# Mixing the first batch's k and v once at full width, in one-bank tiles emptied by two engines, in a new order

## Chip, cores, metric

One core of one Trainium2 chip. The metric is the device time of one execution in microseconds (us); most executions of one kernel agree within 0.3%. An execution is called slow when it is over 1.5% above the fastest of the same kernel, and such executions are left out of every comparison.

Engines in the profile: PE is TensorE (matmuls), PEld its weight loads, DVE is VectorE, ACT is ScalarE, POOL is GpSimd, SP is SyncE. PSUM is the memory that matmuls write, in banks of 512 fp32 columns.

## The reference

Four batches of eight heads, 768 positions, 64 per head. Every head's k and v are mixed over eight blocks of 96 positions by an 8x8 matrix `P` that five rounds of exp and normalisation make; block-local attention follows; its output goes through a bilinear feed-forward part.

```python
for _ in range(5):
    P = np.exp(P - P.max(-1, keepdims=True))
    P = P / P.sum(-1, keepdims=True);  P = P / P.sum(-2, keepdims=True)
k_sorted = einsum('bhij,bhjcd->bhicd', P, k_blocks)     # the same for v
attn = softmax(scale * q_block @ k_sorted_block.T)      # within a block of 96
x = (attn @ v_sorted_block), heads side by side         # [3072, 512]
out = ((x @ w_a) * (x @ w_b)) @ w_out                   # 512 -> 1536 -> 512
```

## The kernel before

The feed-forward matmuls of one batch run while the attention of the next is made in the gaps between them ("units" between "steps"). Only batch 0 has no feed-forward work beside it, so its attention is made in two halves (blocks 0 to 3, then 4 to 7): the first half alone, in the startup; the second half between the first feed-forward steps. Each half mixes k and v of a head pair on its own:

```python
def half_mix(h, hp, what, eng, fill=0, cols=512):       # h: half, hp: pair of heads
    ...
    mix = psF.tile([P, 512], FP32, tag="F", name="mixh")
    keep_busy(mix, fill, cols)                           # filler matmuls
    for c in range(NCH):                                 # 6 chunks of 128 positions
        for e in range(2):                               # the two heads
            nc.tensor.matmul(<64 partitions, 64 columns of mix>,
                lhsT=src2[:, e, c * D:(c + 1) * D],
                rhs=s_all[:, 2 * hp + e, h * NBH:(h + 1) * NBH], start=True, stop=True)
    copy(eng, <kT or vT>, mix)                           # one engine, 128x384

# startup, order on TensorE (cut)
half_mix(0, 0, "k", "act", fill=2, cols=256); half_mix(0, 0, "v", "dve")
to_columns(1)
half_mix(0, 1, "k", "act")
half_scores(0, 0); half_v(0, 0)
half_mix(0, 1, "v", "dve"); half_mix(0, 2, "k", "act", fill=1)
half_o(0, 0); half_scores(0, 1); half_v(0, 1)
...
# second half, between feed-forward steps (cut)
def M(hp): half_mix(1, hp, "k", "act"); half_mix(1, hp, "v", "act")
def R(hp): half_scores(1, hp); half_v(1, hp)
```

`s_all` holds the mixing weights (P times a mask). `half_scores` makes q times k and an Exp on ScalarE, `half_v` turns (transposes) v, `half_o` makes the output and normalises it on VectorE, `half_x` turns that for the feed-forward part. At the end of the startup five "early products" (`begun`) do three of the four accumulations of the first feed-forward tiles, and the first steps only close them. `psF` has four one-bank buffers, `psA` two of two banks. On TensorE, GpSimd and SyncE the program's order is kept; outside the startup the instructions of ScalarE and VectorE are placed by a scheduler.

The softmax here doesn't subtract the row's maximum and nothing guards it: scores larger than these inputs give would overflow.

## Time and profile before

| | before |
|---|---|
| time, median of the first 3 runs | 243.91 us (243.35 to 244.25) |
| span of the profiled run | 241.7 us |
| TensorE busy | 97% of the span, clock full |
| from the permutations' end (`P` is ready and TensorE begins to turn it) to the first closing matmul (startup) | 11.66 us |
| from there to batch 1's first matmul (dense stretch) | 21.43 us |

The table cuts the span where the argument cuts it. TensorE is busy in both stretches; the difference is that in the startup each step waits for the one before it, while in the dense stretch feed-forward matmuls fill whatever time is left. How to read the views, and the lines themselves, are in the prediction.

### The profile page before, as it was taken

The page shows a single profiled execution, that of the slowest core. Times are in us where ns is not written, and L with a number is a line of the kernel's source. Part 1 is how long each engine was busy: PE and PEld are TensorE (multiplying, and loading weights), DVE is VectorE, ACT ScalarE, POOL GpSimd, SP SyncE. Part 2 cuts the span into 40 slices and gives each one's busy share as a digit, 9 for nine tenths or more (in the row PEclk, how much of TensorE's full clock was granted, in tenths as well). Part 3 has the DMA queues.
Part 4 walks back from the last instruction along what each step waited for, and adds up shares of the span by engine and source line. Part 5 has one row for each costly group of instructions (what it writes and reads, how often), then busy time and mean ns, then how long its engine had stood idle before and what let it go on. Part 6 is the DMA issues. An engine that isn't in the chain of part 4 may idle for free.

```text
span 241.7 us, 5392 instructions
## 1 busy us (share of the span) xinstructions
PE 235.4 (97%) x2179; PEld 140.2 (58%) x2189; DVE 109.1 (45%) x258; ACT 104.1 (43%) x198; POOL 70.4 (29%) x97
## 2 busy tenths in 40 slices
PE   7999999999999999999999999999999999999994
PEld 7776666666645466566545455666644465565443
DVE  6775556554436144466416234543544144344110
ACT  2665854566730065744650256455410133333001
POOL 8866559623130045052720516402000000000000
PEclk9999999999999999999999999999999999999999
DMA  5999999984999579869994798962315210000132
GB/s 78 202 200 195 197 200 202 202 139 81 161 183 186 130 73 166 136 111 190 161 199 139 133 234 137 144 131 45 76 47 134 106 43 0 3 0 0 46 129 90
DMA packets 63529, 30.38 MB, mean 126 GB/s; under 512 B 40336, under 2 KB 60560, under 8 KB 63504
## 3 DMA queue, kind: packets, MB, share of 16 engines
q0 software_dynamic: 20944, 14.16, 41.4%
q1 hardware_dynamic: 42416, 15.81, 33.1%
q8 instruction: 17, 0.28, 0.5%
q14 instruction: 8, 0.07, 0.1%
q10 hardware_dynamic: 144, 0.07, 0.1%
HBM read 28.32 MB, written 6.29 MB: 143 GB/s over the span
## 4 chain that ended last, share of the span: by engine, by line
PE 92%; DVE 4%; ACT 1%; DMA 1%; issue 1%; DVEq 0%
PE pf L361 52%; PE po L406 24%; PE o_ps L231 3%; PE sc L331 2%; PE mix L281 2%; PE mixh L180 2%; PE mix L299 2%; PE po L391 1%; PE vs_ps L208 1%; PE xt_ps L222 1%; PE sc L195 1%; DMA p_nat<-in_sort_net_dram 1%; PE two L361 1%; PE heat L168 1%; PE q_ps L260 1%
## 5 line engine op out<-in xcount | busy, mean ns | idle before, releaser
L382 DVE TENSOR_TENSOR hT<-a_sb,pf 128x384 bf16<-128x384 bf16 x95 | 52.6, 554 | 74.2 <-PE pf L361 46.9
L361 PE MATMUL pf<-xT,w_a_sb 128*128 128x384 bf16 x380 | 78.0, 326 | 0.2 <-ACT xT L162 0.2
L361 PE MATMUL pf<-xT,w_b_sb 128*128 128x384 bf16 x380 | 77.5, 326 | 0.0
L381 ACT CAST a_sb<-pf 128x384 bf16<-128x384 f32 x95 | 45.5, 479 | 59.3 <-PE pf L361 36.2
L406 PE MATMUL po<-w_out_sb,hT 128*128 128x512 bf16 x266 | 61.0, 379 | 0.5
L361 PEld LDWEIGHTS <-w_b_sb 128*128 128x128 bf16 x384 | 37.5, 98 | 24.8 <-issue 0.3
L361 PEld LDWEIGHTS <-w_a_sb 128*128 128x128 bf16 x384 | 35.3, 98 | 22.4
L406 PEld LDWEIGHTS <-hT 128*128 128x128 bf16 x276 | 26.3, 98 | 30.1
L162 ACT COPY o_sb<-po 128x512 f32<-128x512 f32 (+1 forms) x13 | 7.5, 578 | 49.0 <-PE po L406 47.5
L164 DVE COPY o_sb<-po 128x512 f32<-128x512 f32 (+1 forms) x12 | 7.9, 658 | 38.5 <-PE po L406 33.9
L336 ACT ACTIVATE eT<-sc 96x768 bf16<-96x768 f32 x24 | 18.1, 802 | 5.2 <-PE sc L331 5.2
L237 DVE TENSOR_TENSOR xp<-o_ps,rec 96x512 bf16<-96x512 f32 x24 | 15.9, 683 | 0.6 <-DVE rec L235 0.2
L318 POOL COPY kT<-turned 128x768 bf16<-128x768 bf16 x6 | 5.0, 827 | 35.0 <-DMA turned<-nat 35.0
L95 POOL DMA_DIRECT2D k<-in_k_dram x16 | 11.6, 725 | 3.2 <-DMA w_a_sb<-in_moe_w_a_dram 1.2
L95 POOL DMA_DIRECT2D v<-in_v_dram x16 | 11.6, 722 | 2.9 <-DMA w_b_sb<-in_moe_w_b_dram 1.3
L231 PEld LDWEIGHTS <-eT 96*128 96x128 bf16 x256 | 10.4, 97 | 3.2 <-DVE xp L237 0.6
L231 PE MATMUL o_ps<-vs,eT 96*128 96x65 bf16 x256 | 11.3, 193 | 0.2 <-DVE xp L237 0.2
L574 POOL COPY gate<-kT 1x1 bf16<-1x1 bf16 x4 | 0.7, 178 | 33.3 <-ACT kT L162 33.3
L162 ACT CAST nat<-mix 128x768 bf16<-128x768 f32 (+1 forms) x12 | 7.7, 639 | 4.2 <-PE mix L299 3.5
L95 POOL DMA_DIRECT2D q<-in_q_dram x12 | 8.7, 724 | 1.9 <-DMA k<-in_k_dram 0.7
L246 POOL COPY qc<-q 128x768 bf16<-128x768 bf16 x10 | 8.4, 841 | 2.4 <-DMA q<-in_q_dram 2.3
L168 PE MATMUL heat<-warm 128*128 128x128 bf16 x84 | 7.6, 264 | 1.3 <-DVE warm L77 1.3
(88 smaller groups left out, 168.6 us busy)
## 6 DMA issues: line engine op xcount, KB each, us to landing
out_dram<-o_sb SPq DMA_DIRECT2D x17, 256.0 KB, 2.0
k<-in_k_dram POOLq DMA_DIRECT2D x16, 192.0 KB, 5.7
v<-in_v_dram POOLq DMA_DIRECT2D x16, 192.0 KB, 6.6
q<-in_q_dram POOLq DMA_DIRECT2D x12, 192.0 KB, 6.6
w_a_sb<-in_moe_w_a_dram POOLq DMA_DIRECT2D x6, 256.0 KB, 9.8
w_b_sb<-in_moe_w_b_dram POOLq DMA_DIRECT2D x6, 256.0 KB, 9.9
w_out_sb<-in_moe_w_out_dram POOLq DMA_DIRECT2D x3, 512.0 KB, 10.6
out_dram<-o_sb SPq DMA_DIRECT2D x12, 128.0 KB, 2.4
```

Source lines behind the costliest of these rows:

```text
L95: nc.gpsimd.dma_start(out=to, in_=_ap(t, base, [[W, P], [S * D, 2], [1, W]]))
L162: nc.scalar.copy(out=out, in_=in_)
L164: nc.vector.tensor_copy(out=out, in_=in_)
L168: nc.tensor.matmul(ps[:, 0:cols], lhsT=warm[:, 0:P], rhs=warm[:, 0:cols], start=True, stop=True)
L231: nc.tensor.matmul(o_ps[:, e, i * (D + 1):(i + 1) * (D + 1)], lhsT=eT[:, hf, e, i * BLK:i * BLK + P], rhs=vs[0:BLK, i0 + i, V0 - 1 + e * ( ...
L237: nc.vector.tensor_tensor(out=_ap(xp, i0 * 2 * D, [[nxp * 2 * D, BLK], [D, 2], [2 * D, NBH], [1, D]]), in0=_ap(o_ps, 1, [[1024, BLK], [511 ...
L246: nc.gpsimd.tensor_copy(out=qc.rearrange("p c e d -> p e c d"), in_=loaded[g][2].rearrange("p e (c d) -> p e c d", c=NCH))
L336: nc.scalar.activation(out=eT[:, hf, :, 0:HB], in_=sc[0:BLK, :, 0:HB], func=AF.Exp, scale=float(scale))
L361: nc.tensor.matmul(pf[:, 0:HW], lhsT=w_sb[:, kc, m * P:(m + 1) * P], rhs=x_cols(b, kc, t), start=(kc == 0), stop=(kc == KA - 1))
L381: nc.scalar.copy(out=a_sb, in_=pf[:, 0:HW])
L382: nc.vector.tensor_mul(out=hT[:, m, t * HW:(t + 1) * HW], in0=a_sb, in1=ab[1][:, 0:HW])
L406: nc.tensor.matmul(held["po"], lhsT=hTs[b][:, m, c * P:(c + 1) * P], rhs=w_out_sb[:, m, :], start=(m == 0), stop=(m == KO - 1))
```

## The change

Intent: mix k and v of batch 0 once, at full width (all eight blocks, 128 columns per matmul), in the startup. The second half then needs no mixing. A mix has 768 columns, more than one bank, so it goes into two one-bank tiles that ScalarE and VectorE empty side by side. The order of the startup, and which engine empties what, came from a search.

```diff
-    def half_mix(h, hp, what, eng, fill=0, cols=512):
...
+    def mix_first(g, what, engines, fill=0, cols=512):
+        mix = [psF.tile([P, 512], FP32, tag="F", name="mixf") for _ in range(2)]
+        keep_busy(mix[0], fill, cols)
+        mix_mms(g, what, lambda c: mix[c // 3][:, c % 3 * P:(c % 3 + 1) * P])
+        for u, eng in enumerate(engines):
+            copy(eng, turned(g, what, u),
+                 _ap(mix[u], 0, [[512, P], [P, 3], [CG, NB], [1, CG]]))
...
             to_columns(0)
-            spread(nc.vector, pc_ps, 0, 2, 0, NBH)
-            spread(nc.vector, pc_ps, 2, 6, 0, NBH)
+            to_columns(1)
+            spread(nc.vector, pc_ps, 0, 2)
+            spread(nc.vector, pc_ps, 2, 2)
+            nc.vector.tensor_copy(out=p_col, in_=pc_ps)
+            spread(nc.gpsimd, p_col, 4, 4)
+            load_ab(1)
...
-            half_mix(0, 0, "k", "act", fill=2, cols=256)
-            half_mix(0, 0, "v", "dve")
-            to_columns(1)
-            half_mix(0, 1, "k", "act")
...
+            mix_first(0, "v", ("act", "dve"), 2, 256)
+            mix_first(0, "k", ("dve", "act"))
+            mix_first(1, "v", ("act", "dve"), 1)
+            mix_first(1, "k", ("act", "dve"))
             half_scores(0, 0)
             half_v(0, 0)
+            mix_first(2, "v", ("act", "dve"))
+            mix_first(2, "k", ("act", "act"))
             half_o(0, 0)
             half_scores(0, 1)
             half_v(0, 1)
+            half_v(0, 2)
+            mix_first(3, "k", ("dve", "act"))
+            half_scores(0, 2)
+            half_o(0, 1)
+            mix_first(3, "v", ("act", "act"))
...
-            us = [lambda: M(0)]
+            us = []
             for hp in range(HP):
-                if hp + 1 < HP:
-                    us.append(lambda hp=hp: M(hp + 1))
                 us.append(lambda hp=hp: R(hp))
...
-                want = s + 1 if s < slow else -(-(s + 1) * len(units) // (n - spare))
+                want = -(-(s + 1 - first) * len(units) // n)
```

Also: four k and four v buffers instead of three, six q buffers instead of eight, the second chunk of `w_a` and `w_b` loaded after GpSimd's `spread` instead of before it, k of later pairs emptied by one ScalarE instruction instead of two, and the early products in another order; besides, one clearing of k's padding less, and two PSUM tiles allocated in the other order.

More of the change, by code (lines that the diff above doesn't have):

```diff
@@ L93, in load_pair @@
                 continue
-            to = ld.tile([P, 2, W], BF16, tag=name, name=name)
+            to = ld.tile([P, 2, W], BF16, tag=name, name=name,
+                         bufs=6 if name == "q2" else None)
             nc.gpsimd.dma_start(out=to, in_=_ap(t, base, [[W, P], [S * D, 2], [1, W]]))
@@ L120 @@
     load_ab(0)
-    load_ab(1)
     mask = const.tile([P, CG], BF16, name="mask")
     NBUF = 3
-    kTs = [const.tile([P, S + PAD], BF16, name=f"kT{n}") for n in range(NBUF)]
-    vTs = [const.tile([P, NB, P], BF16, name=f"vT{n}") for n in range(NBUF)]
+    kTs = [const.tile([P, S + PAD], BF16, name=f"kT{n}") for n in range(HP)]
+    vTs = [const.tile([P, NB, P], BF16, name=f"vT{n}") for n in range(HP)]
     eTs = [const.tile([BLK, 2, 2, HB + PAD], BF16, name=f"eT{n}") for n in range(NBUF)]
@@ L131 @@
         nc.vector.memset(t[:, S:], 0.0)
-        nc.vector.memset(t[:, HB:HB + PAD], 0.0)
     for t in vTs:
@@ L169, in keep_busy, with mix_mms, turned @@
                              start=True, stop=True)
-    def half_mix(h, hp, what, eng, fill=0, cols=512):
-        g = h * HP + hp
-        src2 = loaded[hp][0 if what == "k" else 1]
-        to = (kTs if what == "k" else vTs)[g % NBUF]
-        mix = psF.tile([P, 512], FP32, tag="F", name="mixh")
-        keep_busy(mix, fill, cols)
+    def mix_mms(g, what, where):
+        src2 = loaded[g][0 if what == "k" else 1]
         for c in range(NCH):
             for e in range(2):
-                nc.tensor.matmul(
-                    _ap(mix, e * D * 512 + c * CG, [[512, D], [BLK, NBH], [1, CG]]),
-                    lhsT=src2[:, e, c * D:(c + 1) * D],
-                    rhs=s_all[:, 2 * hp + e, h * NBH:(h + 1) * NBH], start=True, stop=True)
+                nc.tensor.matmul(where(c)[e * D:(e + 1) * D], lhsT=src2[:, e, c * D:(c + 1) * D],
+                                 rhs=s_all[:, 2 * g + e], start=True, stop=True)
+    def mix_first(g, what, engines, fill=0, cols=512):
[5 more added lines that the diff above has]
+                 _ap(mix[u], 0, [[512, P], [P, 3], [CG, NB], [1, CG]]))
+    def turned(g, what, u):
         if what == "k":
-            copy(eng, to[:, 0:HB], mix[:, 0:HB])
-        else:
-            copy(eng, to[:, 0:NBH, 0:BLK], _ap(mix, 0, [[512, P], [BLK, NBH], [1, BLK]]))
+            return _ap(kTs[g % HP], u * 3 * CG, [[S + PAD, P], [CG, 3], [BLK, NB], [1, CG]])
+        return _ap(vTs[g % HP], u * 3 * CG, [[NB * P, P], [CG, 3], [P, NB], [1, CG]])
     def half_scores(h, hp):
         g = h * HP + hp
-        kT, qT, eT = kTs[g % NBUF], st[hp, "qT"], eTs[g % NBUF]
+        kT, qT, eT = kTs[hp], st[hp, "qT"], eTs[g % NBUF]
         sc = psA.tile([P, 2, 512], FP32, tag="A", name="sc")
@@ L196, in half_scores @@
                     sc[:, e, i * BLK:(i + 1) * BLK],
-                    lhsT=kT[e * D:(e + 1) * D, i * BLK:i * BLK + P],
+                    lhsT=kT[e * D:(e + 1) * D, (h * NBH + i) * BLK:(h * NBH + i) * BLK + P],
                     rhs=qT[e * D:(e + 1) * D, :, (h * NBH + i) * CG:(h * NBH + i + 1) * CG],
@@ L204, in half_v @@
         g = h * HP + hp
-        vT, vs = vTs[g % NBUF], vss[g % NBUF]
+        vT, vs = vTs[hp], vss[g % NBUF]
         vs_ps = psF.tile([P, NBH, 2, D], BF16, tag="F", name="vs_ps")
         for i in range(NBH):
-            nc.tensor.matmul(vs_ps[:, i], lhsT=vT[:, i], rhs=ident, is_transpose=True)
+            nc.tensor.matmul(vs_ps[:, i], lhsT=vT[:, h * NBH + i], rhs=ident, is_transpose=True)
         nc.vector.tensor_copy(out=vs[0:BLK, 0:NBH, V0:V0 + P],
@@ L267, in turn_v @@
     def turn_v(g):
-        vT, vs = vTs[g % NBUF], vss[g % NBUF]
+        vT, vs = vTs[g % HP], vss[g % NBUF]
         vs_ps = psF.tile([P, NB, P], BF16, tag="F", name="vs_ps")
@@ L272, in turn_v, with stage_k, stage_v @@
         nc.vector.tensor_copy(out=vs[0:BLK, :, V0:V0 + P], in_=vs_ps[0:BLK])
-    def stage_mix(g, what, engines):
-        src2 = loaded[g][0 if what == "k" else 1]
-        to = (kTs if what == "k" else vTs)[g % NBUF]
-        pitch, whole = (BLK, S + PAD) if what == "k" else (P, NB * P)
+    def stage_k(g):
         mix = psA.tile([P, 2, 512], FP32, tag="A", name="mix")
-        for c in range(NCH):
-            for e in range(2):
-                nc.tensor.matmul(
-                    mix[e * D:(e + 1) * D, c // 3, c % 3 * P:(c % 3 + 1) * P],
-                    lhsT=src2[:, e, c * D:(c + 1) * D],
-                    rhs=s_all[:, 2 * g + e], start=True, stop=True)
-        for hf, eng in enumerate(engines):
-            n = 2 // len(engines)
-            for u in range(n):
-                d1 = _ap(to, (hf + u) * 3 * CG, [[whole, P], [CG, 3], [pitch, NB], [1, CG]])
-                s1 = _ap(mix, (hf + u) * 512, [[1024, P], [P, 3], [CG, NB], [1, CG]])
-                copy(eng, d1, s1)
+        cols = mix.rearrange("p b n -> p (b n)")
+        mix_mms(g, "k", lambda c: cols[:, c * P:(c + 1) * P])
+        nc.scalar.copy(
+            out=_ap(kTs[g % HP], 0, [[S + PAD, P], [CG, NCH], [BLK, NB], [1, CG]]),
+            in_=_ap(mix, 0, [[1024, P], [P, NCH], [CG, NB], [1, CG]]))
+    def stage_v(g):
+        mix = psA.tile([P, 2, 512], FP32, tag="A", name="mix")
+        mix_mms(g, "v", lambda c: mix[:, c // 3, c % 3 * P:(c % 3 + 1) * P])
+        for u, eng in enumerate(("dve", "act")):
+            copy(eng, turned(g, "v", u),
+                 _ap(mix, u * 512, [[1024, P], [P, 3], [CG, NB], [1, CG]]))
     def plain(g):
@@ L308, in stage_plain @@
         st[g, what] = turned
-    def stage(g, what, engines):
-        (stage_plain if plain(g) else stage_mix)(g, what, engines)
     def in_order(g, what):
         if what == "k":
-            to = kTs[g % NBUF][:, 0:S].rearrange("p (i c t) -> p c i t", i=NB, c=NCH)
+            to = kTs[g % HP][:, 0:S].rearrange("p (i c t) -> p c i t", i=NB, c=NCH)
         else:
-            to = vTs[g % NBUF][:, :, 0:BLK].rearrange("p i (c t) -> p c i t", c=NCH)
+            to = vTs[g % HP][:, :, 0:BLK].rearrange("p i (c t) -> p c i t", c=NCH)
         nc.gpsimd.tensor_copy(out=to, in_=st[g, what].rearrange("p c (i t) -> p c i t", i=NB))
@@ L321, in return_v @@
         nc.sync.dma_start_transpose(out=vss[g % NBUF][:, :, V0:V0 + P],
-                                    in_=vTs[g % NBUF].rearrange("p i t -> p (i t)"))
+                                    in_=vTs[g % HP].rearrange("p i t -> p (i t)"))
     def stage_scores(g):
-        kT, qT, eT = kTs[g % NBUF], st[g, "qT"], eTs[g % NBUF]
+        kT, qT, eT = kTs[g % HP], st[g, "qT"], eTs[g % NBUF]
         for hf in range(2):
@@ L433 @@
             p_rep = const.tile([BH, NB * NB, CG // 2], FP32, name="p_rep")
+            heat = psA.tile([P, 2, 512], FP32, tag="A", name="heat")
             pc_ps = psA.tile([P, NB, BH], FP32, tag="A", name="pc_ps")
-            heat = psA.tile([P, 2, 512], FP32, tag="A", name="heat")
             keep_busy(heat[:, 0], 32, P)
@@ L485, with partial @@
             to_columns(0)
-            spread(nc.vector, pc_ps, 0, 2, 0, NBH)
-            spread(nc.vector, pc_ps, 2, 6, 0, NBH)
+            to_columns(1)
[4 more added lines that the diff above has]
+            load_ab(1)
             load_ab(2)
             load_ab(3)
-            half_mix(0, 0, "k", "act", fill=2, cols=256)
-            half_mix(0, 0, "v", "dve")
-            to_columns(1)
-            half_mix(0, 1, "k", "act")
-            nc.vector.tensor_copy(out=p_col, in_=pc_ps)
-            spread(nc.gpsimd, p_col, 0, 8, NBH, NBH)
+            begun = {}
+            def partial(n, *kcs):
+                if n not in begun:
+                    begun[n] = (psF.tile([P, 512], FP32, tag="F", name="pf") if n < 3 else
+                                psA.tile([P, 2, 512], FP32, tag="A", name="two")[:, 0])
+                ab_mms(begun[n], (w_a_sb, w_b_sb)[n % 2], 0, n // 2, 0, kcs)
+            mix_first(0, "v", ("act", "dve"), 2, 256)
+            mix_first(0, "k", ("dve", "act"))
+            mix_first(1, "v", ("act", "dve"), 1)
+            mix_first(1, "k", ("act", "dve"))
             half_scores(0, 0)
             half_v(0, 0)
-            half_mix(0, 1, "v", "dve")
-            half_mix(0, 2, "k", "act", fill=1)
+            mix_first(2, "v", ("act", "dve"))
+            mix_first(2, "k", ("act", "act"))
             half_o(0, 0)
@@ L503 @@
             half_v(0, 1)
-            half_mix(0, 2, "v", "act")
-            half_mix(0, 3, "k", "act", fill=1)
-            half_x(0, 0, "dve")
-            half_o(0, 1)
-            half_scores(0, 2)
-            half_v(0, 2)
-            half_mix(0, 3, "v", "act", fill=1)
-            half_x(0, 1, "dve")
+            half_v(0, 2)
[3 more added lines that the diff above has]
+            mix_first(3, "v", ("act", "act"))
+            half_x(0, 0, "dve")
             half_o(0, 2)
+            half_x(0, 1, "act")
             half_scores(0, 3)
+            partial(0, 0)
             half_v(0, 3)
-            begun = [psF.tile([P, 512], FP32, tag="F", name="pf")]
-            ab_mms(begun[0], w_a_sb, 0, 0, 0, range(2))
-            half_x(0, 2, "act")
+            partial(0, 1)
+            half_x(0, 2, "dve")
             half_o(0, 3)
-            begun += [psF.tile([P, 512], FP32, tag="F", name="pf") for _ in range(2)]
-            begun += [psA.tile([P, 2, 512], FP32, tag="A", name="two")[:, 0] for _ in range(2)]
-            for n, (m, w_sb) in enumerate(((0, w_a_sb), (0, w_b_sb), (1, w_a_sb),
-                                           (1, w_b_sb), (2, w_a_sb))):
-                if n == 3:
-                    half_x(0, 3, "act")
-                ab_mms(begun[n], w_sb, 0, m, 0, range(0 if n else 2, KA - 1))
+            partial(4, 0, 1, 2)
+            partial(2, 0, 1, 2)
+            partial(0, 2)
+            half_x(0, 3, "dve")
+            partial(3, 0, 1, 2)
+            partial(1, 0, 1, 2)
+            begun = [begun[n] for n in range(5)]
         for c in range(4, 6):
@@ L542, in units_half @@
         def units_half():
-            def M(hp):
-                half_mix(1, hp, "k", "act")
-                half_mix(1, hp, "v", "act")
             def R(hp):
@@ L564, in c_ @@
                 turn_q(g)
-            stage(g, "k", ("act",))
-            stage(g, "v", ("dve", "act"))
+            if plain(g):
+                stage_plain(g, "k", ("act",))
+                stage_plain(g, "v", ("dve", "act"))
+            else:
+                stage_k(g)
+                stage_v(g)
             if plain(g):
@@ L573, in c_ @@
                 if g >= 2 * HP - 2:
-                    nc.gpsimd.tensor_copy(out=gate, in_=kTs[g % NBUF][0:1, 0:1])
+                    nc.gpsimd.tensor_copy(out=gate, in_=kTs[g % HP][0:1, 0:1])
                     load_later(g)
@@ L623, with interleave @@
             units[b].append(lambda u=u, g=g, then=then: unit(u, g, then))
-        def interleave(steps, units, spare, slow=0):
-            n, done = len(steps), 0
+        def interleave(steps, units, spare, first):
+            n, done = len(steps) - spare - first, 0
             for s, step in enumerate(steps):
                 step()
-                want = s + 1 if s < slow else -(-(s + 1) * len(units) // (n - spare))
+                want = -(-(s + 1 - first) * len(units) // n)
                 while done < min(want, len(units)):
@@ L648 @@
         steps += [lambda m=m: ffn_ab(0, m, 0) for m in range(3, KO)]
-        interleave(steps, units_half(), 1, 3)
+        interleave(steps, units_half(), 1, 2)
         for b in range(B):
```

## The prediction

> **What bounds the kernel now.** First the page, for the whole span. TensorE works 97% of it at full granted clock, and the chain that ended last runs through TensorE for 92%.
>
> ```profile
> PE 235.4 (97%) x2179; PEld 140.2 (58%) x2189; DVE 109.1 (45%) x258; ACT 104.1 (43%) x198; POOL 70.4 (29%) x97
> PEclk9999999999999999999999999999999999999999
> PE 92%; DVE 4%; ACT 1%; DMA 1%; issue 1%; DVEq 0%
> ```
>
> So TensorE time is the currency: work taken off it where it is dense shortens the run; work moved between the other engines does not, unless TensorE then waits. Second, the stretches: 11.78 us (the permutations are ready) to 23.44 (the first closing matmul of the early products is issued), from there to 44.87 (batch 1 begins), and the rest.
>
> ```profile
> 11.78:23.44 11.66, 11.34 (x221) 7.99 (x222) 7.70 (x19) 6.91 (x13) 8.09 (x11) 1.00 1.41 198
> 23.44:44.87 21.43, 21.33 (x282) 13.36 (x280) 12.37 (x28) 12.51 (x25) 13.53 (x17) 1.00 1.36 200
> 44.87:230.00 185.13, 184.44 (x1490) 105.93 (x1499) 79.63 (x157) 77.12 (x147) 39.10 (x52) 1.00 0.66 113
> ```
>
> Columns: length, then busy time of TensorE, weight loads, VectorE, ScalarE, GpSimd; clock; DMA share; GB/s. TensorE looks full in all three, but in the first it is a chain of short dependent steps, since a short matmul counts about 0.2 us busy and is issued in far less. The change touches the first two stretches. Third, the form groups for the mixing:
>
> ```profile
> L180 PE MATMUL mixh<-s_all,k 128*64 128x64 bf16 x96 | 3.0, 199 | 0.1
> L180 PE MATMUL mixh<-s_all,v 128*64 128x64 bf16 x96 | 3.0, 197 | 0.1
> L281 PE MATMUL mix<-s_all,k 128*64 128x128 bf16 x72 | 3.1, 222 | 0.0
> ```
>
> The means hide the price: the 24 half-width matmuls of a pair are followed by the next group 0.50 us later, 24 full-width ones 0.67 us later. The timeline and the chain in order of time show it:
>
> ```profile
> 28.64 0.38 PE L180 MATMUL mixh<-s_all,k 128*64 128x64 bf16 x12
> 28.85 0.36 PE L180 MATMUL mixh<-s_all,v 128*64 128x64 bf16 x12
> 29.14 0.34 PE L195 MATMUL sc<-qT,kT 64*128 64x96 bf16 x8
> ...
> 51.53 0.67 PE mix L281 x24
> ```
>
> From 28.64 to 29.14 is 0.50; half width buys only a quarter off.
>
> **What the Trainium skill says.** "TensorE: Matmul & The Clock Gate", section "Wait — 56ns, not 53.3ns?": 128 columns warm go start to start in 55.6 ns, and no matmul in under about 25 ns. Here two 64-column halves of the array run side by side, and 12 such pairs in 0.67 us are 56 ns a pair, which agrees; the 64-column pairs take 42 ns, 21 ns a matmul, a little under its floor but far from half. "PSUM — Partial Sum Buffer", section "PSUM bank collisions raise a hardware error": two engines must not touch one bank and quadrant at once. That is why each mix now fills two one-bank tiles: ScalarE and VectorE may empty them together. No run here shows a collision. "VectorE: DVE Perf Modes", section "Why PSUM operands drop a tier": an fp32 PSUM source is read at the lowest rate; the trace has 556 ns for 128x384 on VectorE. "ScalarE: Activation LUTs", section "What ACT_TABLE_LOAD costs": 186 ns plus 0.833 ns a column, 506 ns for 384, neighbours overlapping by 93 ns; the trace has 479 ns, and such copies start about 0.40 us apart.
>
> **The change part by part.**
> Removed: 16 half mixes of 12 matmuls, four pairs of them inside the dense stretch. In the timeline these cost, with the 0.1 us that the turn to 64-column tiles takes after a product: 0.88 (first, with 0.2 of a wait), 0.60, 0.50, 0.60, together 2.58 us. Also two of three 512-column fillers, 0.22 us each.
> Added: 8 full mixes before the first product in place of 8 half ones: 8 x 0.335 - 8 x 0.25 = +0.68 us of TensorE. Net TensorE work: 2.58 - 0.68 + 0.43 = 2.3 us less.
> Moved: 16 evacuations of 128x384 stay 16, but all come before the first product, where 8 were. That is 8 more in the startup: ScalarE 10 (before 5), VectorE 6 (before 3), with VectorE also building the weights of four heads at full width from both column products (about 0.42 us for 256 columns, from 0.288 for 128 and 0.547 for 384). ScalarE's startup load: 10 x 0.40 + 4 x 0.72 + 0.4 = 7.3 us; VectorE's: 0.75 + 0.33 + 6 x 0.47 + 4 x 0.35 + 4 x 0.85 + 3 x 0.3 = 9.6 us. From 12.27 that fits before 23.4, barely.
> I then replayed the instruction order of the changed kernel by hand with these durations (0.04 us from the last matmul's end to a reader, 0.10 us from an evacuation to TensorE). First weights 12.69, so v of pair 0 is mixed from 12.74 (before: k from 12.42). Pair 1's k ends at 14.55, held back by buffers: four one-bank tiles, two a mix. First scores 14.55 (before 13.42), pair 2 mixed 15.4 to 16.1, pair 3's k 17.1, its v 18.1 to 18.5 (before 18.2). Scores of pair 3 at 19.62 (before 19.16), output of pair 3 at 21.09 (before 20.57), early products 21.4 to 23.7. So a loss of over a microsecond at the first scores shrinks to about 0.3 us when the early products are done: 23.75 against 23.44.
> Dense stretch, from there to batch 1: closings 0.82, the fourth product's other half 0.65, ten more steps of 1.30 = 13.0, four scores-and-transposes 4 x 0.51 plus 3 x 0.1 for the turn, four outputs about 1.1, four transposes 0.85, a last 0.1: 18.86. Plus one new wait: the new pacing puts the second half's first scores and first output in one gap, with only 0.23 us of transposes between, so the output waits for an Exp of 0.81 us: about 0.8; and the scores wait some 0.3 for the banks of the early products. Sum about 20.0 to 20.1 (before 21.43): 1.35 us less. Together +0.3 - 1.35 = about -1.0 us.
> Small parts: k of a later pair copied by one ScalarE instruction of 768 columns (about 0.80) where two of 0.482 were, a fourth k and v buffer, six q buffers: all beside a dense TensorE, so nothing. Weight loads are issued up to 3 us later (GpSimd's weight-building now stands ahead of them), but the DMA runs at 200 GB/s throughout with at least four earlier transfers queued, so landings stay.
>
> **The rivals.**
> (a) All TensorE savings arrive, 2.3 us or so: 241.5. For it: dense stretch, work gone. Against it: startup is a chain, the Exp wait is in the order.
> (b) Evacuation bounds the startup. Without overlap between neighbouring copies my replay ends the early products at 24.7, 1.3 us late, and the gain is 0.1 us: 243.8. For it: VectorE's 9.6 of 11 us. Against it: the trace shows the overlaps.
> (c) Weights arrive too late. GpSimd's waits give the landings:
>
> ```profile
> 21.34 0.74 POOL L106 DMA_DIRECT2D w_a_sb<-in_moe_w_a_dram  x1 [0.29 <-DMA w_a_sb<-in_moe_w_a_dram]
> 22.67 0.74 POOL L106 DMA_DIRECT2D w_b_sb<-in_moe_w_b_dram  x1 [0.59 <-DMA w_b_sb<-in_moe_w_b_dram]
> ```
>
> The second weight chunk lands at 21.3 and the new order reads it at 21.4, before it was read at 22.95. If the later issue (14.5 against 11.36) passes through whole, TensorE waits up to 3 us: 246. Against it: the queue is never empty.
> (d) Fewer fillers and more gaps let the clock fall; the page shows 9 in all slices, and gaps of 0.1 to 0.4 us should not change that.
>
> **Range and chances.** 243.91 - 1.0 = 242.9. The order was searched, so I lean slightly to (a): 241.6 to 243.9 holds (a) and (b). Two per cent is 4.9 us, twice all TensorE work removed, so faster by 2% is worth 0.02; slower by 2% needs (c) and more, 0.01.
>
> **What would show it.** 96 mixing matmuls for batch 0 where there were 192, none after 24 us. First scores near 14.6; early products done near 23.75; batch 1 beginning 0.6 to 1.5 us earlier than 44.87; a gap of about 0.8 us before an output near 26 us, put down to ScalarE's Exp. From 45 us on equal lengths. I would be wrong if the early products end after 24.5 (b), if TensorE waits for a weight chunk (c), or if the length after batch 1's start changes by over 0.5 us.

## The result, and the profile after

| | before | changed |
|---|---|---|
| median of 6 runs | 243.7 us (243.19 to 244.25) | 242.17 us (241.92 to 242.52) |
| ratio, 95% interval | 1 | 0.9938 (0.992 to 0.9956) |

A ratio is the mean time of one kernel's fast runs over that of the other's fast runs of the same rounds, so it is not quite the ratio of the medians. The gain is 1.5 us, 0.6%: the same within 2%, and inside the predicted range, 0.7 us under the predicted 242.9.

The page of the changed kernel: TensorE's share is as high as before, with 88 matmuls fewer in the count (the program has 98 fewer: 96 of mixing and two fillers; some records are missing from a trace), and the clock is full throughout.

```profile
PE 234.4 (97%) x2091; PEld 139.5 (58%) x2091; DVE 111.3 (46%) x262; ACT 101.1 (42%) x187; POOL 70.4 (29%) x97
PEclk9999999999999999999999999999999999999999
```

Busy share therefore says nothing of the gain; the stretches do. The same three as in the prediction, each cut at the same event (columns as there):

```profile
12.21:24.22 12.01, 11.58 (x219) 8.45 (x220) 9.80 (x24) 7.55 (x16) 8.87 (x12) 1.00 1.41 197
24.22:43.97 19.75, 19.09 (x187) 11.78 (x186) 12.39 (x28) 9.25 (x17) 13.17 (x17) 1.00 1.36 199
43.97:230.00 186.03, 185.81 (x1503) 106.36 (x1503) 79.63 (x157) 76.87 (x142) 39.10 (x52) 1.00 0.69 114
```

Startup 12.01 against 11.66 us (0.35 longer, VectorE 9.8 busy against 7.7), dense stretch 19.75 against 21.43 (1.68 shorter), together 1.33. From batch 1's first matmul to the end of the span both runs take the same to 0.1 us: 240.8 - 43.97 and 241.7 - 44.87 are both about 196.8. This profiled run began its startup 0.43 us later than the one of before (12.21 against 11.78) for a reason that is not the change's (see the end of this section); it was the slowest of the six, 242.52. The control below was cut in the same way at 11.72, 23.73 and 43.48, with stretches of 12.01 and 19.75 again.

The mixing matmuls by form: 48 and 48 at full width, where 96 and 96 at half width were, and each mean is about 0.22 us (0.20 at half width) although they are issued every 28 ns on average.

```profile
L175 PE MATMUL mixf<-s_all,k 128*64 128x128 bf16 x48 | 2.1, 220 | 0.0
L175 PE MATMUL mixf<-s_all,v 128*64 128x128 bf16 x48 | 2.1, 222 | 0.2 <-DVE s_all L153 0.2
```

The timeline of the dense stretch, at its first attention unit, shows what the new pacing costs. Columns: start, duration, engine, line, operation, then in brackets the idle time before it and what ended it.

```profile
25.87 0.35 PE L197 MATMUL sc<-qT,kT 64*128 64x96 bf16 x8
26.15 0.40 PE L210 MATMUL vs_ps<-ident,vT 128*128 128x128 bf16 x4
26.32 0.81 ACT L202 ACTIVATE eT<-sc 96x768 bf16<-96x768 f32 x1 [0.49 <-PE sc L197]
27.18 0.42 PE L233 MATMUL o_ps<-vs,eT 96*128 96x65 bf16 x8 [0.63 <-ACT eT L202]
27.44 0.81 PE L357 MATMUL pf<-xT,w_a_sb 128*128 128x384 bf16 x4
```

Scores at 25.87, next product at 27.44: 1.57 us for work that takes 0.77 when nothing waits (0.28 scores, 0.23 transposes, 0.26 output). The loss is 0.80 us; the idle time in brackets is only 0.63, because it is counted from the modelled end of the transposes, 0.17 us after the last of them stopped holding TensorE up.

One more thing varies from run to run, in both kernels: the pace of TensorE in the first microseconds. Ahead of the turn of the first q stand 16 filler matmuls, and ScalarE's copy of that turned q stands ahead of an Exp of the permutations. The 16 fillers, before and after:

```profile
5.21 1.46 PE L168 MATMUL heat<-warm 128*128 128x128 bf16 x16
5.06 1.89 PE L167 MATMUL heat<-warm 128*128 128x128 bf16 x16
```

In the control they took 1.07. In the records of single matmuls they are issued 107 ns apart until about 6.1, 7.2 and (control) 5.2 us and 56 ns apart from then on, although the clock line shows full all the while. The first q itself was not late: it landed 4.9 us after its issue in both profiled runs. So in the profiled run of the changed kernel the copy waited until 7.58:

```profile
7.58 0.80 ACT L161 COPY qT<-q_ps 128x768 bf16<-128x768 bf16 x1 [1.41 <-PE q_ps L262]
8.27 0.25 ACT L434 ACTIVATE p_nat<-p_nat 32x64 f32<-32x64 f32 x1
8.55 0.21 DVE L447 TENSOR_REDUCE rsum<-p_nat 32x8 f32<-32x64 f32 x1 [0.92 <-ACT p_nat L434]
```

In the profiled run of before the copy began at 7.17 and the Exp at 7.86. That is 0.41 of the 0.43 us.

### The profile page after: what moved, and what is told of

It reads as the page before. It is cut to its first block, busy times and chain, and to the rows that moved or that the text cites. A ratio compares the mean times of both kernels' runs of the same rounds, so it can differ in the third digit from the quotient of the medians.

```text
span 240.8 us, 5193 instructions
## 1 busy us (share of the span) xinstructions
PE 234.4 (97%) x2091; PEld 139.5 (58%) x2091; DVE 111.3 (46%) x262; ACT 101.1 (42%) x187; POOL 70.4 (29%) x97
## 4 chain that ended last, share of the span: by engine, by line
PE 93%; DVE 3%; ACT 1%; DMA 1%; issue 0%; DVEq 0%; ACTq 0%
PE pf L357 52%; PE po L402 24%; PE o_ps L233 3%; PE sc L327 2%; PE mix L175 2%; PE mix L298 2%; PE mixf L175 1%; PE po L387 1%; PE sc L197 1%; PE vs_ps L210 1%; PE heat L167 1%; PE xt_ps L224 1%; DMA p_nat<-in_sort_net_dram 1%; PE q_ps L262 1%; PE two L357 1%; DVE xp L239 1%
## 5 line engine op out<-in xcount | busy, mean ns | idle before, releaser
L402 PE MATMUL po<-w_out_sb,hT 128*128 128x512 bf16 x276 | 61.9, 379 | 0.0
```

The source lines that it names most:

```text
L402: nc.tensor.matmul(held["po"], lhsT=hTs[b][:, m, c * P:(c + 1) * P], rhs=w_out_sb[:, m, :], start=(m == 0), stop=(m == KO - 1))
```

## The experiments

Theory 1, from the prediction: time taken off TensorE in the dense stretch is the gain, less a longer startup and an Exp wait. Rivals: ScalarE's relief is the gain; the order alone, or the split of the emptying alone, is; the buffers are; late weights hold it back. The changed kernel ran again as control. Fast runs only, and the ratio is to the kernel before.

| run | median us | ratio (95%) |
|---|---|---|
| changed, first measurement | 242.17 | 0.9938 (0.992 to 0.9956) |
| changed, control | 242.05 | 0.9939 (0.9926 to 0.9953) |
| matmuls put back | 244.6 | 1.0033 (1.0019 to 1.0046) |
| copies put back | 242.59 | 0.9953 (0.994 to 0.9965) |
| output later | 241.26 | 0.9897 (0.9881 to 0.9913) |
| old order, one engine a mix | 243.19 | 0.9978 (0.9965 to 0.9991) |
| searched order, one engine a mix | 243.17 | 0.9987 (0.9968 to 1.0006) |
| old order, split | 243.4 | 0.9993 (0.9979 to 1.0006) |
| weights loaded as before | 242.28 | 0.995 (0.9929 to 0.9971) |
| no fillers | 241.91 | 0.9937 (0.9918 to 0.9956) |
| output later, q turned later | 241.62 | 0.9919 (0.99 to 0.9937) |
| output later, no fillers | 241.17 | 0.99 (0.9885 to 0.9916) |
| before, new buffers | 243.8 | 1.0006 (0.9986 to 1.0026) |

**Control.** No edit.

> The changed kernel once more, as the control of this call on the same chip: within 0.3 us of its first measurement, 241.9 to 242.5 us.

242.05 us, as expected.

**The second half's matmuls put back, their results unused.**

```diff
+        def again(hp):          # 2 x 12 matmuls of 64 columns, as half_mix(1, hp, ...) had
+            ...                 # into a psF tile that nothing reads
+        for s, hp in ((0, 0), (1, 1), (3, 2), (5, 3)):
+            steps[s] = also(steps[s], again, hp)
```

> The changed kernel with the second-half mixing matmuls put back where they stood in the dense stretch (8 groups of 12 with 64 columns), their results thrown away, no evacuation added. Theory 1 (TensorE time is the currency of the dense stretch): 8 x 0.25 plus three or four turns of 0.1 = 2.3 us more than the changed kernel, so about 244.5 us, slower than the kernel before. Rival (the gain is that ScalarE is relieved of its copies in the dense stretch): no more than 0.3 us, about 242.4.

244.6 us: 2.4 more than the changed kernel's first measurement (2.3 by the two ratios), where 2.3 was expected, with no evacuation put back. So the matmuls alone are worth more than the whole gain, and the rival (ScalarE's relief) falls. The profiled execution is not read for times; its order shows that the wait for the Exp is still there, since the matmuls were put back before the scores and not between them and the output.

**The second half's copies put back, without matmuls.**

```diff
+        def again(hp):
+            for what in range(2):
+                nc.scalar.copy(out=q_first[:, 2 * hp + what, 0:HW], in_=warm[:, 0:HW])
```

> The changed kernel with eight extra ScalarE copies of 128x384 in the dense stretch at the places of the removed evacuations, into dead memory, no matmul added. Theory 1: ScalarE is off the path there, so within 0.3 us of the changed kernel (242.2). Rival (ScalarE's relief is the gain): 8 x 0.40 = up to 3 us of ScalarE, of which 1 us or more shows: 243.3 or more.

242.59 us, 0.4 more than the changed kernel and outside what theory 1 allowed. But the trace shows that it did not test what it was meant to. The added copies by source line:

```profile
L654 ACT COPY q_first<-warm x8: 493/506/514, 6.8 to 13.6; 128x384 bf16<-128x384 bf16 x8
```

They depend on nothing but the turning of q, so the scheduler moved all eight from the dense stretch (from 24 us on) to the startup, 6.8 to 13.6 us. There they stood before copies that matter: cut as above, the startup took 12.27 us (11.83 to 24.10) instead of 12.01, and the dense stretch 19.75 as in the changed kernel. What it says instead: ScalarE time in the startup is not free. What ScalarE's copies cost in the dense stretch is left to the run before this one.

**The second half's first output one step later.**

```diff
-                want = -(-(s + 1 - first) * len(units) // n)
+                want = (0, 0, 1, 2, 4, 5, 7, 8, 10, 11, 12, 12)[s]
```

> The changed kernel with the first output of the second half moved one product step later, so that a step of 1.3 us lies between its scores and it. Theory 1: the wait of 0.63 us for the Exp before that output goes, nothing else moves: about 241.55 us, 0.6 less than the changed kernel. Rival (the wait is taken up again by a buffer or by a later wait in the same stretch): within 0.2 us of the changed kernel, 242.1.

The list of steps moves two more units by one step, the scores of the second and of the third pair; the text of the expectation names only the output. 241.26 us: 0.8 to 0.9 less than the changed kernel, more than the 0.6 that I had read from the bracket. The stretches:

```profile
11.62:23.64 12.02, 11.59 (x219) 8.46 (x220) 9.80 (x24) 7.56 (x16) 8.52 (x11) 1.00 1.41 197
23.64:42.59 18.95, 18.91 (x186) 11.65 (x184) 12.36 (x28) 9.25 (x17) 13.48 (x17) 1.00 1.37 199
```

The startup is the same; the dense stretch is 0.80 us shorter, and only 0.04 us of it is idle. A product of 1.3 us now lies between the scores and the output:

```profile
25.30 0.35 PE L197 MATMUL sc<-qT,kT 64*128 64x96 bf16 x8
25.57 0.40 PE L210 MATMUL vs_ps<-ident,vT 128*128 128x128 bf16 x4
25.74 0.81 ACT L202 ACTIVATE eT<-sc 96x768 bf16<-96x768 f32 x1 [0.49 <-PE sc L197]
25.81 0.81 PE L357 MATMUL pf<-xT,w_a_sb 128*128 128x384 bf16 x4
26.46 0.81 PE L357 MATMUL pf<-xT,w_b_sb 128*128 128x384 bf16 x4
...
27.11 0.41 PE L233 MATMUL o_ps<-vs,eT 96*128 96x65 bf16 x8
```

So the wait was real, of the size that the prediction had worked out (0.8), and removable. The two other moved units can hardly account for it: the bracket shown above is 0.63 of the 0.66 us for which TensorE was idle in the changed kernel's dense stretch.

**Full width, old order, one engine a mix.**

```diff
-            mix_first(0, "v", ("act", "dve"), 2, 256)
-            mix_first(0, "k", ("dve", "act"))
-            ...                                        # the searched order
+            mix_first(0, "k", ("act", "act"), fill=2, cols=256)
+            mix_first(0, "v", ("dve", "dve"))
+            mix_first(1, "k", ("act", "act"))
+            ...                                        # the order of before, three long fillers
```

> Full width alone: the changed kernel's full-width mixing in the order of the kernel before up to the early products, each mix emptied by one engine (k by ScalarE, v by VectorE for pairs 0 and 1 and by ScalarE for pairs 2 and 3), three long fillers as before. Theory 1 with the searched order and the split mattering: ScalarE has 12 copies against 10 and no pair of halves is emptied side by side, so the early products end 1 to 1.5 us later than in the changed kernel and most of the gain is lost: 243.2 to 243.7 us. Rival (only the TensorE work matters, the order is worth little): 242.2 to 242.6.

243.19 us: 1.0 us of the gain gone, at the lower edge of the range of theory 1 with the order and the split mattering. Full width by itself gains 0.2% over the kernel before.

**Searched order, one engine a mix.**

```diff
-            mix_first(0, "v", ("act", "dve"), 2, 256)
-            mix_first(0, "k", ("dve", "act"))
+            mix_first(0, "v", ("dve", "dve"), 2, 256)
+            mix_first(0, "k", ("act", "act"))             # and so for all eight mixes
```

> The changed kernel in its searched order, with each mix emptied by one engine: both k tiles by ScalarE, both v tiles by VectorE (8 and 8 copies instead of 10 and 6). Theory 1 (emptying a mix side by side shortens the chain of the startup): each mix is ready about 0.4 us later, and VectorE, which is the fuller engine, gets two more copies of 0.47 us: 0.5 to 1.2 us slower than the changed kernel, 242.7 to 243.4. Rival (only the order matters, not the split): within 0.2 us, 242.0 to 242.4.

243.17 us: 1.0 us slower than the changed kernel, so the split matters in this order. The profiled run was the slowest of six (243.95), with the second load of q landing about 1.4 us late (9.5 instead of 8.1) and TensorE waiting for later loads of v, so no line of it is used.

**Old order, split.**

```diff
-            mix_first(0, "k", ("act", "act"), fill=2, cols=256)
-            mix_first(0, "v", ("dve", "dve"))
+            mix_first(0, "k", ("act", "dve"), fill=2, cols=256)
+            mix_first(0, "v", ("act", "dve"))             # and so for all eight mixes
```

> Full width in the order of the kernel before, each mix emptied side by side by ScalarE and VectorE (8 copies each). Full width in that order with one engine a mix gave 243.23, and the searched order with one engine a mix 243.17, so both lack the same 1.0 us. Theory: the split alone is that 1.0 us, and this gives 242.2 to 242.6. Rival: split and order are needed together (a mix that is ready sooner helps only if something useful comes next), and this stays at 242.9 to 243.3.

243.4 us: the theory that the split alone is the missing 1.0 us falls, and the rival holds. The stretches:

```profile
11.70:25.04 13.34, 12.53 (x220) 8.82 (x222) 10.44 (x25) 7.69 (x14) 9.10 (x12) 1.00 1.41 197
25.04:44.78 19.74, 19.08 (x186) 11.78 (x184) 12.39 (x28) 9.25 (x17) 12.94 (x17) 1.00 1.36 200
```

The dense stretch is the changed kernel's; the startup is 1.33 us longer, which is the whole difference. Two of the waits in it, from the timeline:

```profile
14.03 0.34 PE L197 MATMUL sc<-qT,kT 64*128 64x96 bf16 x8
...
21.84 0.20 PEld L224 LDWEIGHTS <-xph 96*128 96x128 bf16 x4 [0.62 <-DVE xph L239]
...
22.75 0.32 PE L357 MATMUL pf<-xT,w_a_sb 128*128 128x384 bf16 x1 [0.18 <-ACT xT L161]
```

Its first scores come 2.33 us after the permutations, where the changed kernel needs 2.91 (12.21 to 15.12). Yet at the end it is behind: pair 3's v is mixed late, the turn of pair 2's output waits for VectorE, and two more long fillers (0.22 us each) stand in the order. How the 1.33 us divide among these was not taken apart.

**Weights loaded as before.**

```diff
     load_ab(0)
+    load_ab(1)
...
             spread(nc.gpsimd, p_col, 4, 4)
-            load_ab(1)
             load_ab(2)
```

> The changed kernel with the second weight chunk's loads issued again where the kernel before issued them, ahead of GpSimd's building of the mixing weights. If the later issue of that chunk costs nothing because the transfers are queued anyway (my reading), this gives nothing back, and GpSimd's building for pairs 2 and 3 comes later: it waits for v of pair 1 to land near 13.6, so it ends near 15.5 instead of 14.9; pair 2 is mixed from 15.7 in the changed kernel, so within 0.3 us of it: 242.0 to 242.5 us. Rival (the second chunk arrives late in the changed kernel, and TensorE waits for it at the early products): faster by 0.5 us or more, below 241.7.

242.28 us, no gain: the late issue costs nothing. In the control's trace the second chunk of `w_a` lands as it did before, at 21.04 (before: 21.06); GpSimd's next load, which waits for it, starts 0.28 later:

```profile
21.32 0.74 POOL L107 DMA_DIRECT2D w_a_sb<-in_moe_w_a_dram  x1 [0.60 <-DMA w_a_sb<-in_moe_w_a_dram]
```

In the control TensorE first reads that chunk at 21.36, so there are about 0.3 us of slack.

**No fillers.**

```diff
-            mix_first(0, "v", ("act", "dve"), 2, 256)
+            mix_first(0, "v", ("act", "dve"))
...
-            mix_first(1, "v", ("act", "dve"), 1)
+            mix_first(1, "v", ("act", "dve"))
```

> The changed kernel without its three fillers (two of 256 columns, one of 512). TensorE waits there for the mixing weights and for banks anyway: 0 to 0.2 us faster, 242.0 to 242.2, if the clock stays at full; if the fillers hold the clock up, the granted clock falls in the startup and it is slower by 0.5 us or more.

241.91 us: 0.1 to 0.3 less by the medians, but its ratio is that of the changed kernel, so not told apart from it. The granted clock stays at full: with TensorE as busy as it is here, the fillers are not needed for it.

**Output later, q turned later.**

```diff
-                if it == 2:
-                    turn_q(0, "act")
                 if it == 3:
-                    turn_q(1, "act")
+                    turn_q(0, "act")
                 if it == 4:
+                    turn_q(1, "act")
                     turn_q(2, "act")
-                    turn_q(3, "act")
...
             to_columns(1)
+            turn_q(3, "act")                  # and no first fillers; the later output as above
```

> The version meant to beat both: the changed kernel with the first output of the second half moved one step later (as in the run before, 241.26), and the four turns of q moved one iteration later, the last of them into the place of the first fillers, so that ScalarE's copy of the first one, which waits for the load of q, no longer stands ahead of an Exp of the permutations. In the trace of the changed kernel that copy started at 7.58 and held the Exp up by about 0.4 us; in the run with the later output it started at 6.78 and held up nothing. So 0 to 0.4 us less than 241.26: 240.9 to 241.3. If the extra evacuation in the startup delays the first mix, 241.5 or more.

A miss: 241.62, slower than the later output alone by the medians (the intervals overlap). The turn of q that I put in the place of the fillers keeps ScalarE until 13.39, and the first mix, ready about 0.3 us earlier, waits for it:

```profile
12.59 0.80 ACT L161 COPY qT<-q_ps 128x768 bf16<-128x768 bf16 x1 [0.81 <-PE q_ps L262]
...
13.28 0.48 ACT L161 CAST vT<-mixf 128x384 bf16<-128x384 f32 x1
```

First scores come 3.21 us after the permutations (11.71 to 14.92) against 2.91, and the whole startup takes 12.31 against 12.02 with the later output alone. The premise was wrong too: in the changed kernel's run the first copy of q waited for TensorE's fillers (see the profile after), not for the load.

**Output later, no fillers.**

```diff
-                want = -(-(s + 1 - first) * len(units) // n)
+                want = (0, 0, 1, 2, 4, 5, 7, 8, 10, 11, 12, 12)[s]
...                                            # and the fillers' diff of above
```

> The version meant to beat both, second try: the changed kernel with the first output of the second half one step later and without the three fillers; q is left where it was. The first alone gave 241.26 and the second alone 241.91, so 0.2 to 0.3 us less than the first: 241.0 us (240.8 to 241.3) if the two add up. If the time is bound by the landing of k and v of pairs 2 and 3 rather than by TensorE, the second adds nothing: 241.3.

241.17 us, the fastest, but its interval (0.9885 to 0.9916) covers the ratio of the later output alone (0.9897): the fillers are worth about 0.1 us, if anything. Both versions beat both kernels: 1.0% under the kernel before, 0.4% under the changed one.

**The kernel before, with the new buffers.**

```diff
-    kTs = [... for n in range(NBUF)]
-    vTs = [... for n in range(NBUF)]
+    kTs = [... for n in range(HP)]            # 4; every index by g % HP; six q buffers
+    vTs = [... for n in range(HP)]
```

> The kernel before with the changed kernel's buffers alone: four k and four v tiles in place of three, six q tiles in place of eight. TensorE is dense where they are used, so 0: within 0.3 us of the kernel before, a ratio of 0.999 to 1.001. Rival: waits for k and v buffers were part of what was saved: 243.2 or less, a ratio under 0.998.

A ratio of 1.0006: nothing. The buffers are needed to hold four pairs at once; as such they save no time.

## Why the prediction was right

- *TensorE time in the dense stretch, 2.58 us removed.* Right: the stretch is 1.68 us shorter with the new wait of 0.80 in it, so about 2.5 were removed; put back alone, the matmuls cost 2.3 to 2.4.
- *A half-width matmul saves only a quarter.* True of a group with the pause after it, not of a matmul. In the lines of the prediction the first 12 take 0.21 us and the last 12, with the pause before the scores, 0.29. In the records of single matmuls a pair of 64 columns follows the last every 32 ns (not 42) and a pair of 128 every 56. The 0.50 us holds a pause of about 0.1 at the change of tile shape and the 0.67 holds none; with its own, the full group took 0.71 (51.42 to 52.13). So two half mixes of k and v cost 1.0 us where one full one costs 0.71, in part because they pay that pause twice. The estimate of the time removed stands, as it was read from starts in the timeline.
- *Startup 0.3 us longer.* Right: 0.35. From the permutations to the first closing matmul 12.01 us were measured and 11.97 predicted (23.75 - 11.78); to the first scores 2.91 against 2.77, to the output of pair 3 9.41 against 9.31. So the replay was right on the way and not only at its end. The hand replay had to count that neighbouring copies overlap; rival (b), without overlap, is out by 0.9 us.
- *Exp wait of 0.8 us.* Right: 0.80, removed by the later output.
- *Scores wait 0.3 us for the banks of the early products.* This term was too large: scores came 1.65 us after the first closing matmul, where 1.57 was the work with its turn, so 0.08. The dense stretch was predicted at about 20.05 and measured at 19.75; this term is 0.22 of the difference, and the larger part of the gap between -1.0 and the -1.33 of the traces. The remaining 0.2 to the 1.5 of the medians is within what the start of the run varies by.
- *Weights arrive as before (rival c out).* Right: same landing, and no gain from the earlier issue; the margin, about 0.3 us, is thinner than the words "landings stay" suggest.
- *Buffers and small parts nothing, clock full (rival d out).* Right for the buffers and the clock, by a run each. The single ScalarE copy of later k was not tried by itself; from batch 1 on both traces take the same time.
- *Slips in the working, without effect on the sum.* In the startup of before ScalarE emptied 6 mixes and VectorE 2, not 5 and 3, so VectorE's share grew more than was said. The 12.27 from which VectorE's load is counted is in no trace; in the changed kernel VectorE began 0.41 us after the permutations, which would be 12.19. The "fourth product" of the dense stretch is the third.
- *What I had not seen:* that the order and the split are worth about 1 us only together. The prediction took both as given.

## What to carry to other kernels

Where one engine is dense, count the start-to-start time of what leaves it, not its mean duration, and count the pauses where the shape of the tiles changes: here a group of 24 half-width matmuls cost 0.50 us and one of full width 0.71, so doing the work once at full width paid even though it moved to a stage that is bound by latency. Then look for what the removal leaves side by side: here a producer and its consumer, formerly kept apart by the work that left, met with 0.23 us between them and lost 0.80 to an Exp, and one product put between them gave that back. Splitting an evacuation over two engines and reordering the work around it had to be tried together; each alone gained nothing over the old order with one engine.

## What the Trainium skill lacked or had wrong

- "TensorE: Matmul & The Clock Gate", section "Wait — 56ns, not 53.3ns?": it says that start to start never drops below about 25 ns. Matmuls that alternate between the two 64-column halves of the array go faster: 12 of 64 columns were issued in 0.21 us (28.64 to 28.85 in the trace of before, 17.5 ns each), the two of a pair 3 to 4 ns apart. The page's own section "Measured speedup vs the span model" has about 4 ns a tile, which agrees. What the page lacks is the time from pair to pair, 32 ns at 64 columns and 56 at 128, and that of the pause before matmuls of another tile shape, about 0.1 us here.
- The same page, section "Seeing it yourself", ties the reduced clock to a third busy core on a die and names 13/16 (0.81) of full speed. Two executions of these one-core programs were held at 0.75 and 0.85 from 10 us to the end (means 0.757 and 0.851), in 306.14 and 273.53 us instead of 244.6 and 243.2. Neither is 13/16; the runs do not show what else the die was doing.
- "ScalarE: Activation LUTs", section "What ACT_TABLE_LOAD costs": its formula gives 506 ns for 384 columns. The copies out of SBUF in the run with copies put back took 506 ns in the median, as it says; the same size out of PSUM took 479 ns, which the formula does not separate.
- "Perfetto Trace Analysis", section "Tensor Engine Instruction (MATMUL, LD_WEIGHTS)": it says that the reported end is estimated, but not what that does to idle times. Here an idle time of 0.63 us before a matmul stood for 0.80 us of lost issue time.
- No page has how much the first loads of an execution vary. The second load of q landed 5.7 us after its issue in the profiled run of the changed kernel and 7.1 us after it in that of the weights loaded as before; GpSimd's eighth load of k or v waited for it for 0.25 us in the one and 1.74 us in the other.
